# A fused retention and feed-forward kernel: v of chunk 0 loaded and cast by GpSimd's queue, q and k by the two hardware queues, and attention products issued batch by batch instead of grouped in pairs by tiling mode

## Chip, cores, metric

One core of one Trainium2 chip. The metric is the device time of the kernel in microseconds; lower is better. The engines are called as in the profile: PE is TensorE, DVE VectorE, ACT ScalarE, POOL GpSimd, SP SyncE, which here only issues DMAs.

## What is computed

```python
# q, k, v: (4, 8, 768, 64) float32; w_in: (512, 2048); w_out: (2048, 512)
gamma = 1.0 - 2.0 ** (-5.0 - np.arange(H))
for t in range(S):
    state = gamma * state + einsum('bhd,bhe->bhde', k[:, :, t], v[:, :, t])
    y[:, :, t] = scale * einsum('bhd,bhde->bhe', q[:, :, t], state)
x = y.transpose(0, 2, 1, 3).reshape(B * S, H * D)      # 3072 tokens x 512
h = x @ w_in
g = 0.5 * h * (1 + tanh(c * (h + 0.044715 * h ** 3)))  # gelu
out = g @ w_out                                        # 3072 x 512 float32
```

## The kernel before

The recurrence over 768 steps is cut into 6 chunks (index c) of 128 steps, for 4 batches (b). The 8 heads stand as 4 pairs (NHP = 4) of 64 + 64 columns. For a chunk and a batch the work is:

- Load: q, k, v come as 128 x 8 x 64 float32, 256 KB each, in rows of 256 B (load1, L76). prep1 (L135) makes float16 of them: q and k by a product with a decay column, v by a cast.
- T: mm_T (L178) transposes q and k of the 4 pairs by 8 plain 128x128 products into one PSUM bank, and ev_T (L187) copies it to SBUF.
- A: mm_A (L192) makes k q^T per head: 8 products with 64 rows of contraction each, "64*128" in the profile, the two heads of a pair on the two halves of the array's rows, into two banks. ev_A (L206) multiplies both by a decay mask on DVE.
- Y: the carry products (mm_yc, L213) multiply q by the state, 4 plain products; the inner products (mm_yi, L228) multiply A by v, 8 products of 64 columns each, "128*64", the two heads on the two halves of the array's columns, into the same bank. ev_Y (L241) copies it to xT, the transposed input of the feed-forward part.
- S: mm_s (L246), 4 plain products k^T v, and ev_S (L259), which adds the decayed state; decay (L275) is a product on POOL.

The feed-forward part of a chunk takes all 512 tokens. moe1 (L361) makes one block of 128 hidden units with 4 products over the contraction, then a gelu on ACT; moe1_two (L366) puts two blocks of at most 256 tokens into one bank and gives both to one gelu. In chunks 0 and 1, where the tokens of only some batches are there yet, moe1_two is used on 128 or 256 tokens at a time. moe2 (L385) accumulates 16 products per batch into one bank; ev_O (L390) copies it out and stores it, for the last batch by DVE and SP, for the others by ACT.

The order is written out by hand, and each engine runs its instructions in that order. PSUM's 8 banks are shared by tags: "h" 2, "o" 2, "att" 4 (L173). A tile is given a bank of its tag that is free in program order.

- Chunk 0 is written line by line (L427 to L493), with spin (L109), products on zeros, between the pieces. The loads of its 12 tiles are spread over SP and ACT (L90 to L100, L427, L428, L435). w_in is loaded by POOL's queue, which casts it to float16, right behind the k product of batch 2 (L452); hold (L86) keeps the loads of chunk 1 back until a block of w_in is there.
- Chunk 1's attention stands among the feed-forward units of chunks 0 and 1 (L533 to L568).
- From chunk 2 on, run (L417) calls the units of a stage and, after given units, the pieces of attention listed for them. att_AY (L294) groups two batches: carry products of both, A of the next two batches, inner products of both. The S products come later, by att_S.

```python
for b in bs:   mm_yc(c, b, tag)
for b in abs_: mm_A(ca, b)
for b in bs:   mm_yi(c, b)
```

Of the kernel before, what the change touches and what calls it, by code (L numbers as in the profile page):

```python
# [16 lines left out]
def kernel(  # L17
# [37 lines left out]
    att = ctx.enter_context(tc.tile_pool(name="att", bufs=4))  # L55
# [34 lines left out]
    nc.sync.dma_start(out=cst[:, :OT + 128], in_=cst_h.ap())  # L90
    load1(nc.scalar, "q", 0, 0)
    load1(nc.sync, "k", 0, 0)
    load1(nc.scalar, "v", 0, 0)
# [3 lines left out]
    load1(nc.sync, "v", 0, 1)  # L97
    load1(nc.sync, "k", 0, 2)
    load1(nc.sync, "q", 0, 3)
    load1(nc.sync, "v", 0, 3)  # L100
# [8 lines left out]
    def spin(n):  # L109
        ps = bank("o", shape=(128, 512), name="spin_ps")  # L110
        for _ in range(n):
            nc.tensor.matmul(  # L112
                out=ps, lhsT=zero[:, 0:128], rhs=zero, start=True, stop=True
            )
# [3 lines left out]
    nc.gpsimd.memset(st, 0.0)  # L118
# [13 lines left out]

    h16 = {}
# [37 lines left out]


    BANKS = {"h": 2, "o": 2, "att": 4}  # L173

    def bank(tag, dt=F32, shape=(128, NHP, 128), name="ps"):
        return psum.tile(list(shape), dt, tag=tag, bufs=BANKS[tag], name=name)

    def mm_T(c, b):  # L178
        ps = bank("att", F16, (128, 2, NHP, 128), "qkT_ps")
        for i, nm in ((0, "q"), (1, "k")):  # L180
            for hp in range(NHP):
                nc.tensor.transpose(  # L182
                    out=ps[:, i, hp], in_=pair(h16[nm, c, b], hp), identity=iden
                )
        pss["T", c, b] = ps
# [6 lines left out]
    def mm_A(c, b):  # L192
        t = qkT[c, b]
        ps = [bank("att", name=f"a_ps{j}") for j in range(2)]
# [18 lines left out]
    def mm_yc(c, b, tag):  # L213
        y_ps = pss["Y", c, b] = bank(tag, name="y_ps")
        if c == 0:
            return

        for hp in range(NHP):
            nc.tensor.matmul(  # L219
                out=y_ps[:, hp],  # L220
                lhsT=st[:, hp, b],
                rhs=qkT[c, b][:, 0, hp],
                start=(hp == 0),
                stop=False,
                skip_group_check=True,
            )

    def mm_yi(c, b):  # L228
        y_ps = pss["Y", c, b]
        for hp in range(NHP):  # L230
            for j in range(2):
                nc.tensor.matmul(  # L232
                    out=y_ps[j * 64:(j + 1) * 64, hp],
                    lhsT=h16["v", c, b][:, 2 * hp + j],
                    rhs=a_sb[c, b, j][:, hp],
                    start=(c == 0),
                    stop=True,
                    skip_group_check=True,
                )

# [5 lines left out]
    def mm_s(c, b, tag="att"):  # L246
        if c + 1 >= NCk:
            return
        s_ps = pss["S", c, b] = bank(tag, name="s_ps")
        for hp in range(NHP):  # L250
            nc.tensor.matmul(  # L251
                out=s_ps[:, hp],
                lhsT=pair(h16["k", c, b], hp),
                rhs=pair(h16["v", c, b], hp),
                start=True,
                stop=True,
            )

    def ev_S(c, b, eng=nc.vector):  # L259
# [3 lines left out]
        for j in range(2):  # L263
            sl = slice(j * 64, (j + 1) * 64)
            if c == 0:
                copy_on(eng, st[sl, :, b, sl], s_ps[sl, :, sl])
            else:
                eng.tensor_tensor(  # L268
# [15 lines left out]
    def att_T(c, *bs):  # L284
        for b in bs:
            mm_T(c, b)
            ev_T(c, b)

    def att_S(c, b, tag="att"):
        mm_s(c, b, tag)  # L290
        ev_S(c, b)
        decay(c, b)

    def att_AY(c, bs, tag, ca, abs_, eng):  # L294


        for b in bs:
            mm_yc(c, b, tag)
        for b in abs_:
            mm_A(ca, b)  # L300
        for b in bs:
            mm_yi(c, b)
        if tag == "o":
            for b in abs_:
                ev_A(ca, b)
        for b in bs:
            ev_Y(c, b, eng)
        if tag != "o":
            for b in abs_:
                ev_A(ca, b)  # L310
# [30 lines left out]
    def moe1_mm(c, fc, out, t0, t1):  # L341
        wi, wr = w_in_of[fc]
        for kc in range(NHP):
            nc.tensor.matmul(  # L344
                out=out,
# [4 lines left out]
                skip_group_check=True,  # L350
            )

    def g_tile(c, fc):
        if (c, fc // 2) not in g_sb:
            g_sb[c, fc // 2] = gp.tile([128, 2, B * C], F16, tag=f"g{fc // 2}", name="g")
        return g_sb[c, fc // 2]

    def gelu(out, in_):
        nc.scalar.activation(out=out, in_=in_, func=AF.Gelu_apprx_tanh, scale=1.0)  # L359

    def moe1(c, fc):  # L361
        h_ps = bank("h", shape=(128, B * C), name="h_ps")
        moe1_mm(c, fc, h_ps, 0, B * C)
        gelu(g_tile(c, fc)[:, fc % 2], h_ps)

    def moe1_two(c, fp, t0, t1):  # L366

        h_ps = bank("h", shape=(128, 2, B * C // 2), name="h_ps")
        for r in range(2):
            moe1_mm(c, 2 * fp + r, h_ps[:, r, 0:t1 - t0], t0, t1)  # L370
        gelu(g_tile(c, 2 * fp)[:, :, t0:t1], h_ps[:, :, 0:t1 - t0])
# [3 lines left out]
    def moe2_mm(ps, c, b, fcs, n0, n1):  # L375
        for fc in fcs:
            nc.tensor.matmul(  # L377
                out=ps[:, n0:n1],
                lhsT=g_sb[c, fc // 2][:, fc % 2, b * C:(b + 1) * C],
# [5 lines left out]
    def moe2(c, b, fcs):  # L385
        if fcs[0] == 0:
            o_ps[c, b] = bank("o", shape=(128, d_model), name="o_ps")
# [13 lines left out]
    def moe2_last(c, b):  # L401
# [4 lines left out]
        for i in range(2):  # L406
            ps = bank("h", shape=(128, d_model), name="o_ps")
# [9 lines left out]
    def run(units, after):  # L417
        for i, u in enumerate(units):
            u()
            for f, *args in after.get(i, ()):  # L420
                f(*args)
# [5 lines left out]
    load1(AC, "q", 0, 2)  # L427
    load1(AC, "v", 0, 2)  # L428
# [3 lines left out]
    prep1(AC, "v", 0, 0)  # L432
# [10 lines left out]
    prep1(AC, "v", 0, 1)  # L443
    spin(2)
    mm_yc(0, 0, "o")
    mm_yi(0, 0)
    mm_s(0, 0, "h")
# [13 lines left out]
    ev_T(0, 2, AC)  # L461
    prep1(VE, "q", 0, 3)
    mm_yc(0, 1, "o")
    mm_yi(0, 1)
    mm_s(0, 1, "h")
    ev_Y(0, 1, AC)
    prep1(AC, "v", 0, 2)
    prep1(AC, "v", 0, 3)
    ev_S(0, 0, AC)
# [5 lines left out]
    mm_yc(0, 2, "o")  # L475
    mm_yi(0, 2)
    mm_s(0, 2)
    ev_Y(0, 2, AC)
    ev_S(0, 1, AC)
    mm_A(0, 3)  # L480
    ev_A(0, 3)
    moe1_two(0, 0, 0, half)
    mm_yc(0, 3, "o")
    mm_yi(0, 3)
    mm_s(0, 3)
# [3 lines left out]
    moe1_two(0, 1, 0, half)  # L489
    for fp in range(2):  # L490
        moe1_two(0, fp, half, 2 * half)
# [8 lines left out]
    for b in range(B):  # L500
        load1(SY, "q", 1, b)
        load1(SY, "k", 1, b)

# [13 lines left out]


    def att_A(c, b):
        mm_A(c, b)  # L520
        ev_A(c, b)

    def att_Y(c, b):
        mm_yc(c, b, "o")
        mm_yi(c, b)
        mm_s(c, b, "o")
        ev_Y(c, b, AC)

    def end_S(c, b):
        ev_S(c, b)  # L530
        decay(c, b)

    att_T(1, 0)  # L533
    moe1(0, NF - 1)
    prep1(AC, "v", 1, 0)
    att_A(1, 0)
    spin(3)
    att_Y(1, 0)
    att_T(1, 1)
    end_S(1, 0)  # L540
    moe1_two(1, 0, 0, C)
    prep1(AC, "v", 1, 1)
    att_A(1, 1)
    for fp in range(1, 4):
        moe1_two(1, fp, 0, C)
    att_Y(1, 1)
    moe1_two(1, 4, 0, C)
    prep1(AC, "v", 1, 2)
    moe1_two(1, 0, C, half)
    att_T(1, 2)  # L550
    end_S(1, 1)
    moe1_two(1, 1, C, half)
    att_A(1, 2)
    moe1_two(1, 2, C, half)
    moe1_two(1, 3, C, half)
    prep1(AC, "v", 1, 3)
    att_Y(1, 2)
    moe1_two(1, 4, C, half)
    att_T(1, 3)
    end_S(1, 2)  # L560
    moe1_two(1, 5, 0, half)
    att_A(1, 3)
    moe1_two(1, 6, 0, half)
    moe1_two(1, 7, 0, half)
    att_Y(1, 3)
    end_S(1, 3)
    for fp in range(NF // 2):
        moe1_two(1, fp, half, 2 * half)  # L568


    def units2(c, b, n=4):
        u = [(lambda i=i: moe2(c, b, range(i, i + n))) for i in range(0, NF, n)]
        last = u[-1]
        u[-1] = lambda: (last(), ev_O(c, b))
        return u

    for b in range(B):
        prep(2, b)
    u = [units2(0, b, NF // 2) for b in range(B)]
    run(  # L580
        [u[0][0], u[1][0], u[0][1], u[1][1], u[2][0], u[3][0], u[2][1], u[3][1]],
        {
            1: [(att_T, 2, 0), (load, 3, 0)],
            2: [(att_T, 2, 1), (load, 3, 1)],
            4: [(att_AY, 0, (), "o", 2, (0, 1), None), (load, 3, 2)],
            5: [(att_T, 2, 2), (load, 3, 3)],
            6: [(att_T, 2, 3)],
        },
    )
    for b in range(B):  # L590
        prep(3, b)
    run(
        [x for b in range(B) for x in units2(1, b)],
        {
            1: [(att_AY, 2, (0, 1), "h", 2, (2, 3), AC)],
            4: [(att_S, 2, 0), (load, 4, 0)],
            5: [(att_S, 2, 1), (load, 4, 1)],
            7: [(att_T, 3, 0)],
            8: [(att_T, 3, 1), (load, 4, 2)],
            10: [(att_AY, 2, (2, 3), "h", 3, (0, 1), AC), (load, 4, 3)],  # L600
            12: [(att_S, 2, 2)],
            13: [(att_S, 2, 3)],
        },
    )

    for c in range(2, NCk - 1):
        n = c + 1
        more = n + 1 < NCk
        after = {
            1: [(att_T, n, 2)],  # L610
            3: [(att_T, n, 3)],
            8: [(att_AY, n, (0, 1), "o", n, (2, 3), VE)],
            11: [(att_S, n, 0)],
# [55 lines left out]
```

## Time and profile before

| | us |
|---|---|
| median of 3 runs | 223.31 (223.24, 223.31, 224.55) |
| the profiled execution | 224.55 |
| its span in the profile | 222.8 |
| PE busy | 212.7 (95%) |
| ACT busy | 87.9 (39%) |
| POOL busy | 78.9 (35%) |
| DVE busy | 71.9 (32%) |
| first feed-forward product starts | 18.20 |
| first product with w_out starts | 57.23 |

The span is cut into stages by what PE does: attention of chunk 0 to 18.2 us; the first product (w_in) of chunk 0 to 34.3; the attention and first product of chunk 1 to 57.2; the second product (w_out) of chunk 0 to about 75; that of chunk 1, in which most of chunk 2's attention stands, to 92.8; then one stage per chunk of some 33.7 us, 31.4 where no attention follows. In the profile, a line of the timeline is a run of equal instructions: start, time from the first start to the last end, engine, source line, operands, number. Ends of matmuls are modelled, so work is read from start to start.

### The profile page before, as it was taken

To read this page: it belongs to the slowest core of one execution; us is meant where nothing else is said; L and a number is where in the kernel's file an instruction comes from. 1 tells how busy PE (TensorE), PEld (TensorE's weight loads), DVE (VectorE), ACT (ScalarE), POOL (GpSimd) and SP (SyncE) were. 2 spreads that over 40 slices of the span, in tenths; PEclk is the share of its full clock that TensorE was granted. 3 is DMA by queue.
4 is the path that set the end of the run, shared out by engine and by line. 5 is a ranking of instruction groups with operands and counts; after the bars stand their busy time and mean duration, and the time that the engine had idled before them with its cause. 6 is when DMAs were issued, how large, how long until landed. Compare 5 with 4: busy or idle time off the path is not lost.

```text
span 222.8 us, 4048 instructions
## 1 busy us (share of the span) xinstructions
PE 212.7 (95%) x1667; PEld 118.8 (53%) x1667; DVE 71.9 (32%) x132; ACT 87.9 (39%) x154; POOL 78.9 (35%) x91
## 2 busy tenths in 40 slices
PE   7697998899999999999999999999999999999993
PEld 3356446778645556555455555455455445444452
DVE  3466016551025445526324425323425100100001
ACT  2384665655312122254512255512154513367120
POOL 3493365709876770660750794000000000000000
PEclk9999999999999999999999999999999999999999
DMA  7999999999999999999811110011110011200112
GB/s 168 288 190 207 207 264 207 143 190 226 240 240 283 237 297 244 270 258 225 181 50 47 47 47 3 0 50 47 47 49 3 0 47 50 96 0 0 47 50 94
DMA packets 83011, 29.74 MB, mean 133 GB/s; under 512 B 75568, under 2 KB 80048, under 8 KB 82992
## 3 DMA queue, kind: packets, MB, share of 16 engines
q1 hardware_dynamic: 65776, 17.94, 34.4%
q0 software_dynamic: 4224, 4.19, 11.8%
q10 hardware_dynamic: 12992, 7.34, 10.8%
q8 instruction: 13, 0.21, 0.4%
q14 instruction: 6, 0.05, 0.1%
HBM read 27.37 MB, written 6.29 MB: 151 GB/s over the span
## 4 chain that ended last, share of the span: by engine, by line
PE 81%; DMA 8%; SPq 4%; DVE 2%; ACT 1%; issue 1%; POOL 0%; ACTq 0%; DVEq 0%
PE h_ps L344 36%; PE o_ps L377 33%; PE qkT_ps L182 4%; SPq L77 4%; DMA k<-in_k_dram 3%; PE y_ps L232 3%; DMA w_in<-in_moe_w_in_dram 3%; PE a_ps L197 2%; DMA q<-in_q_dram 2%; PE s_ps L251 2%; PE y_ps L219 2%; DVE a_sb L210 1%; DMA out_dram<-o_sb 1%; ACT g L359 1%; POOL k L145 0%
## 5 line engine op out<-in xcount | busy, mean ns | idle before, releaser
L344 PE MATMUL h_ps<-xT,w_in 128*128 128x512 f16 (+2 forms) x504 | 88.2, 329 | 1.6 <-DMA w_in<-in_moe_w_in_dram 1.2
L377 PE MATMUL o_ps<-w_out,g 128*128 128x512 f16 (+1 forms) x400 | 87.7, 371 | 0.3 <-ACT o_sb L398 0.3
L359 ACT ACTIVATE g<-h_ps 128x512 f16<-128x512 f32 (+1 forms) x101 | 58.1, 576 | 55.7 <-PE h_ps L344 55.6
L344 PEld LDWEIGHTS <-w_in 128*128 128x128 f16 x504 | 45.2, 98 | 36.3 <-DMA w_in<-in_moe_w_in_dram 1.4
L377 PEld LDWEIGHTS <-g 128*128 128x128 f16 x400 | 37.9, 98 | 39.0 <-issue 0.3
L210 DVE TENSOR_TENSOR a_sb<-a_ps,mask 128x512 f16<-128x512 f32 x48 | 30.2, 684 | 31.4 <-PE a_ps L197 31.3
L169 DVE COPY qkT<-qkT_ps 128x1024 f16<-128x1024 f16 x21 | 14.5, 691 | 51.1 <-PE qkT_ps L182 51.1
L145 POOL TENSOR_TENSOR k<-k,cst 128x512 f16<-128x512 f32 x24 | 25.3, 1056 | 11.8 <-DMA k<-in_k_dram 11.8
L398 ACT COPY o_sb<-o_ps 128x512 f32<-128x512 f32 x18 | 10.5, 585 | 47.6 <-PE o_ps L377 44.0
L277 POOL TENSOR_TENSOR stg<-st,cst 128x512 f32<-128x512 f16 x16 | 16.4, 1037 | 26.0 <-DVE st L268 25.9
L145 POOL TENSOR_TENSOR q<-q,cst 128x512 f16<-128x512 f32 x20 | 20.9, 1044 | 6.0 <-DMA q<-in_q_dram 4.5
L167 ACT CAST xT<-y_ps 128x512 f16<-128x512 f32 x17 | 9.5, 588 | 17.4 <-PE y_ps L232 13.0
L268 DVE TENSOR_TENSOR st<-s_ps,stg 64x256 f16<-64x256 f32 x32 | 13.5, 421 | 7.5 <-PE s_ps L251 6.9
L395 DVE COPY o_sb<-o_ps 128x512 f32<-128x512 f32 x5 | 3.5, 691 | 23.3 <-PE o_ps L377 23.3
L182 PEld LDWEIGHTS <-q 128*128 128x128 f16 x96 | 7.2, 98 | 6.0 <-issue 0.9
L182 PE MATMUL qkT_ps<-iden,q 128*128 128x128 f16 x96 | 9.3, 219 | 0.9 <-DMA iden<-rr_ident 0.6
L142 POOL CAST v<-v 128x512 f16<-128x512 f32 x16 | 9.8, 609 | 0.9 <-DMA v<-in_v_dram 0.8
L182 PE MATMUL qkT_ps<-iden,k 128*128 128x128 f16 x96 | 9.3, 220 | 0.7 <-POOL k L145 0.7
L232 PE MATMUL y_ps<-a_sb,v 128*64 128x128 f16 x192 | 9.3, 223 | 0.7 <-DVE a_sb L210 0.5
L112 PE MATMUL spin_ps<-zero 128*128 128x512 f16 x27 | 8.3, 445 | 1.2 <-DVE zero L104 1.2
L197 PE MATMUL a_ps<-qkT 64*128 64x128 f16 x192 | 8.2, 218 | 1.2 <-DVE qkT L169 0.7
L411 DVE COPY o_sb<-o_ps 128x256 f32<-128x256 f32 x1 | 0.4, 424 | 25.2 <-PE o_ps L377 25.2
(29 smaller groups left out, 76.0 us busy)
## 6 DMA issues: line engine op xcount, KB each, us to landing
k<-in_k_dram SPq DMA_DIRECT2D x22, 256.0 KB, 4.6
q<-in_q_dram SPq DMA_DIRECT2D x22, 256.0 KB, 4.5
v<-in_v_dram SPq DMA_DIRECT2D x18, 256.0 KB, 4.7
out_dram<-o_sb ACTq DMA_DIRECT2D x18, 256.0 KB, 2.0
w_in<-in_moe_w_in_dram POOLq DMA_DIRECT2D x4, 512.0 KB, 8.6
w_out<-in_moe_w_out_dram POOLq DMA_DIRECT2D x4, 512.0 KB, 9.3
v<-in_v_dram ACTq DMA_DIRECT2D x6, 256.0 KB, 5.5
out_dram<-o_sb SPq DMA_DIRECT2D x5, 256.0 KB, 2.0
```

The costliest lines, as they stand in the source:

```text
L145: eng.tensor_tensor(out=t, in0=src, in1=cst[:, col:col + H].unsqueeze(2).broadcast_to([128, H, Dh]), op=ALU.mult,)
L169: eng.tensor_copy(out=out, in_=in_)
L182: nc.tensor.transpose(out=ps[:, i, hp], in_=pair(h16[nm, c, b], hp), identity=iden)
L197: nc.tensor.matmul(out=ps[j][:, hp], lhsT=t[j * 64:(j + 1) * 64, 1, hp], rhs=t[j * 64:(j + 1) * 64, 0, hp], start=True, stop=True,)
L210: nc.vector.tensor_tensor(out=s, in0=ps[j], in1=mask[:, j], op=ALU.mult)
L232: nc.tensor.matmul(out=y_ps[j * 64:(j + 1) * 64, hp], lhsT=h16["v", c, b][:, 2 * hp + j], rhs=a_sb[c, b, j][:, hp], start=(c == 0), stop=True,
L268: eng.tensor_tensor(out=st[sl, :, b, sl], in0=s_ps[sl, :, sl], in1=stg[sl, :, b, sl], op=ALU.add,)
L277: nc.gpsimd.tensor_tensor(out=stg[:, :, b], in0=st[:, :, b], in1=cst[:, OG:OG + NHP].unsqueeze(2).broadcast_to([128, NHP, 128]), op=ALU.mult,)
L344: nc.tensor.matmul(out=out, lhsT=w_in_sb[wi][:, kc, wr * 128:(wr + 1) * 128], rhs=xT[c][:, kc, t0:t1], start=(kc == 0), stop=(kc == NHP - ...
L359: nc.scalar.activation(out=out, in_=in_, func=AF.Gelu_apprx_tanh, scale=1.0)
L377: nc.tensor.matmul(out=ps[:, n0:n1], lhsT=g_sb[c, fc // 2][:, fc % 2, b * C:(b + 1) * C], rhs=w_out_sb[fc // (NF // NO)][:, fc % (NF // NO ...
L398: nc.scalar.copy(out=o_sb, in_=ps)
```

## The change

- Chunk 0's v is loaded by POOL's queue straight into float16 tiles (load_v16), four issues on POOL; the four loads of v on SP and ACT and the four casts on ACT go. The loads of q and k of chunk 0 are dealt anew over SP and ACT, and the memset of st moves from POOL to DVE.
- Attention is issued batch by batch: mm_Y holds carry, inner and S products of one batch; A is a piece of its own. From chunk 2 on, std lists twelve pieces per chunk, and zip_units spreads them evenly over the units.
- moe1_two goes: each block of 128 hidden units has its own bank and gelu, in chunks 0 and 1 on 128 or 256 tokens.
- Banks: "h" 3, "o" 2, "att" 3. In chunk 0, the S products of batches 0 to 2 take "h" banks and are copied by DVE; from chunk 2 on y and S take "att" banks and ev_Y runs on DVE. The pool of transposed q and k has 3 buffers instead of 4.
- Chunk 2's attention no longer stands in chunk 0's second product, only in chunk 1's. The loads of chunks 3 and later are issued at other places.

```diff
-    att = ctx.enter_context(tc.tile_pool(name="att", bufs=4))
+    att = ctx.enter_context(tc.tile_pool(name="att", bufs=3))
...
+    def load_v16(c, b):
+        t = h16["v", c, b] = pre.tile([128, H, Dh], F16, tag="v16", name="v16")
+        nc.gpsimd.dma_start(
+            out=t, in_=srcs["v"][b, :, c * C:(c + 1) * C, :].rearrange("h p d -> p h d")
+        )
     load1(nc.scalar, "q", 0, 0)
     load1(nc.sync, "k", 0, 0)
-    load1(nc.scalar, "v", 0, 0)
+    load_v16(0, 0)
     nc.sync.dma_start(out=iden, in_=iden_h.ap())
     load1(nc.sync, "q", 0, 1)
     load1(nc.scalar, "k", 0, 1)
-    load1(nc.sync, "v", 0, 1)
+    load_v16(0, 1)
+    load1(nc.scalar, "q", 0, 2)
     load1(nc.sync, "k", 0, 2)
+    load_v16(0, 2)
     load1(nc.sync, "q", 0, 3)
-    load1(nc.sync, "v", 0, 3)
...
-    nc.gpsimd.memset(st, 0.0)
+    nc.vector.memset(st, 0.0)
...
+    def mm_Y(c, b):
...
+        att_b, o_b, h_b = ("att", 3), ("o", 2), ("h", 3)
+        tag, bufs = o_b if c < 2 else att_b
+        y_ps = psum.tile([128, NHP, 128], F32, tag=tag, bufs=bufs, name="y_ps")
...
+        if c + 1 < NCk:
+            tag, bufs = (h_b if b < 3 else att_b) if c == 0 else (o_b if c == 1 else att_b)
+            s_ps = psum.tile([128, NHP, 128], F32, tag=tag, bufs=bufs, name="s_ps")
...
+    def att_Y(c, b):
+        mm_Y(c, b)
+        ev_Y(c, b)
         ev_S(c, b)
         decay(c, b)
...
+    def moe1(c, fc, t0=0, t1=B * C):
+        h_ps = psum.tile([128, B * C], F32, tag="h", bufs=3, name="h_ps")
...
-    def moe1_two(c, fp, t0, t1):
...
+        todo = pieces(c, "T0 T1 A0 T2 A1 Y0 T3 A2 Y1 A3 Y2 Y3")
+        if c + 1 < NCk:
+            for at, b in ((8, 0), (10, 1), (12, 2), (14, 3)):
+                todo.insert(at, ("P", c + 1, b))
...
+    def zip_units(units, todo, over=None):
+        over = len(units) if over is None else over
+        done = 0
+        for i, u in enumerate(units):
+            u()
+            want = min(len(todo), ((i + 1) * len(todo) + over - 1) // over)
+            while done < want:
+                nm, c, b = todo[done]
+                fn[nm](c, b)
+                done += 1
...
     spin(14)
     prep1(VE, "q", 0, 0)
     prep1(PO, "k", 0, 0)
-    prep1(AC, "v", 0, 0)
+    load_v16(0, 3)
...
+    ev_S(0, 0)
     prep1(VE, "q", 0, 3)
-    mm_yc(0, 1, "o")
-    mm_yi(0, 1)
-    mm_s(0, 1, "h")
+    mm_Y(0, 1)
     ev_Y(0, 1, AC)
-    prep1(AC, "v", 0, 2)
-    prep1(AC, "v", 0, 3)
-    ev_S(0, 0, AC)
     mm_A(0, 2)
     ev_A(0, 2)
...
     mm_A(0, 3)
     ev_A(0, 3)
-    moe1_two(0, 0, 0, half)
+    ev_S(0, 1)
+    moe1(0, 0, 0, half)
+    moe1(0, 1, 0, half)
+    mm_Y(0, 3)
     ev_Y(0, 3)
     ev_S(0, 2)
     ev_S(0, 3)
-    moe1_two(0, 1, 0, half)
-    for fp in range(2):
-        moe1_two(0, fp, half, 2 * half)
+    for fc in range(2, 4):
+        moe1(0, fc, 0, half)
+    for fc in range(4):
+        moe1(0, fc, half, 2 * half)
...
+    units = [(lambda fc=fc: moe1(1, fc, C, half)) for fc in range(10)]
+    units += [(lambda fc=fc: moe1(1, fc, 0, half)) for fc in range(10, NF)]
+    units.insert(8, lambda: prep1(AC, "v", 1, 3))
+    zip_units(units, pieces(1, "T2 s1 A2 y2 T3 s2 A3 y3 s3"))
+    for fc in range(NF):
+        moe1(1, fc, half, 2 * half)
...
+    zip_units([u for b in range(B) for u in units2(1, b)], std(2), 15)
+    for c in range(2, NCk):
+        if c + 2 < NCk:
+            for b in range(B):
+                load(c + 2, b)
+        units = [(lambda fc=fc: moe1(c, fc)) for fc in range(NF)]
+        if c + 1 < NCk:
+            units += [u for b in range(B) for u in units2(c, b)]
+            zip_units(units, std(c + 1), len(units) - 2)
```

In std and zip_units, T, A and Y stand for the pieces of a batch and P for its prep; the lower-case y and s of chunk 1 are Y with its copy on ACT, and S's eviction with the decay.

## The prediction

> **What bounds the kernel now.** I read the engine totals and the 40 slices of the page first, then the waits, then TensorE's timeline. All times are of the profiled execution.
>
> ```profile
> PE 212.7 (95%) x1667; PEld 118.8 (53%) x1667; DVE 71.9 (32%) x132; ACT 87.9 (39%) x154; POOL 78.9 (35%) x91
> PE   7697998899999999999999999999999999999993
> ...
> PEclk9999999999999999999999999999999999999999
> DMA  7999999999999999999811110011110011200112
> ...
> PE 81%; DMA 8%; SPq 4%; DVE 2%; ACT 1%; issue 1%; POOL 0%; ACTq 0%; DVEq 0%
> ```
>
> TensorE is busy in all but about 10 us, at full clock, and the chain that ended last is TensorE for 81%. The gaps lie early. These lines of TensorE's timeline give the start and duration of each piece, and the idle time before it in brackets:
>
> ```profile
> 18.20 1.05 PE L344 MATMUL h_ps<-xT,w_in 128*128 128x256 f16 x8 [1.20 <-DMA w_in<-in_moe_w_in_dram]
> ...
> 44.34 0.38 PE L232 MATMUL y_ps<-a_sb,v 128*64 128x128 f16 x7 [0.30 <-DVE a_sb L210]
> ...
> 46.76 0.40 PE L197 MATMUL a_ps<-qkT 64*128 64x128 f16 x8
> 47.09 1.92 PE L344 MATMUL h_ps<-xT,w_in 128*128 128x256 f16 x16
> ...
> 49.16 0.41 PE L232 MATMUL y_ps<-a_sb,v 128*64 128x128 f16 x8
> 49.51 0.40 PE L251 MATMUL s_ps<-v,k 128*128 128x128 f16 x4
> 50.25 7.15 PE L344 MATMUL h_ps<-xT,w_in 128*128 128x256 f16 x64 [0.35 <-ACT xT L167]
> ...
> 67.77 1.89 PE L377 MATMUL o_ps<-w_out,g 128*128 128x512 f16 x8 [0.29 <-ACT o_sb L398]
> ```
>
> So the first product of the feed-forward part waits for w_in until 18.20; from there TensorE idles for about 2.5 us in all, the last time 0.29 us at 67.77. After that only TensorE's own work counts, and in it the order of the attention products:
>
> ```profile
> 101.45 0.61 PE L219 MATMUL y_ps<-qkT,st 128*128 128x128 f16 x8
> 101.99 0.62 PE L197 MATMUL a_ps<-qkT 64*128 64x128 f16 x16
> 102.54 0.64 PE L232 MATMUL y_ps<-a_sb,v 128*64 128x128 f16 x16
> 103.11 2.76 PE L344 MATMUL h_ps<-xT,w_in 128*128 128x512 f16 x12
> 105.71 0.39 PE L251 MATMUL s_ps<-v,k 128*128 128x128 f16 x4
> 105.94 1.89 PE L344 MATMUL h_ps<-xT,w_in 128*128 128x512 f16 x8
> ```
>
> Read the starts. A plain 128-column product takes 0.22/4 = 0.056 us (s_ps: 105.71 to 105.94), a 512-column one 0.216. The 16 row-tiled A products run two at a time, so 8 x 0.056 = 0.445 us are their work, and they take 0.55; the 16 column-tiled Y products take 0.57 for the same 0.445; and the way into A costs 0.54 - 0.445. So each change of the tiling costs about 0.11 us. The single pieces of chunk 1 say the same: A from 46.76 to 47.09 is 0.33 for 0.22 of work, Y from 49.16 to 49.51 is 0.35 for 0.22.
>
> **What the Trainium skill says.** "TensorEngine Tiling (Array Packing)", section Key Properties: changing the tiling mode, not just the tile, drains the array. The trace agrees, with 0.11 us each. "DMA: Bandwidth & Descriptors", section Issuing engines are not separate DMA queues: all issuers share the same 16 engines; the trace shows these engines full (9) from 5.6 us on. The same page, section Specifications: below 512 B a transfer is under line rate, with read-modify-write; no run here shows a casting load of 256 B rows into 128 B rows. "SBUF — State Buffer", section SBUF: two separate sides: descriptors that GpSimd writes can starve while VectorE holds their shared port; the trace has no such case that I can separate.
>
> **The change, part by part.**
>
> *Attention products by batch (chunks 2 to 5).* The matmuls stay the same in number and shape; only their order changes. Before, two batches stand together: carry products (plain), A of the next pair (rows), inner products (columns), then plain again: 3 changes. There are seven such groups, one with A alone (2) and a last one without A (2): 25 changes. After, each of the 16 batches has A by itself (2 changes) and Y by itself (carry plain, inner by columns, S plain: 2), so 64. 39 more x 0.11 = 4.4 us (0.09 to 0.125 each gives 3.5 to 4.9). All of it is on TensorE, and nothing hides it.
>
> *Do the evictions keep up with 3 att banks instead of 4?* In chunks 3 to 5 one piece comes about every two units of 0.86 us; a piece asks VectorE for 0.69 (T), 1.29 (A, the pair) or 0.69 + 0.86 = 1.55 us (Y and S), all under 1.73. The densest stage is chunk 2, whose 12 pieces all stand in the 16 units of chunk 1's second product, one per unit. I followed it by these durations: T0 and T1 at 0.9 and 1.3 us of the stage, their copies done at 2.1 and 2.8; A0 starts at 2.6 with both banks free, its evictions end at 4.4; A1 at 5.2 needs that bank: free; Y0 at 6.6 has its S bank at 6.4; A2 at 9.6 has its banks at 7.9 and 8.7. No wait. Sum of VectorE there: 15 us of 21. Cost 0.
>
> *Chunk 0: one hidden block at a time.* The h banks go from 2 to 3, but s_ps of batches 0, 1 and 2 now sit in all three, and only batch 0's is evicted when the first product asks (ev_S(0, 1) comes after ev_A(0, 3) on VectorE). So moe1(0, 0) and moe1(0, 1) share one bank, and so does moe1(0, 2); all of TensorE's queue stands behind that wait. With 0.43 us for a 256-column unit and 0.384 us for its gelu (row 128x256), from the first product: unit 0 ends at 0.55, its gelu at 1.03, unit 1 at 1.51, Y(0, 3) at 2.1, then six units, the third and fourth of them again one gelu behind: 4.8 us. Before the same work ends at 4.16 (1.57 + 6 x 0.432). +0.65.
>
> *Chunk 1: single units of 128 columns.* Their gelu is estimated at 0.28 us (0.384 minus half of 0.597 - 0.384) against 0.22 us of TensorE. Scalar's work in the stage grows from 14.0 to 17.6 us, TensorE has some 20. The waits for a_sb keep their times (Y(1, 2) at 44.3, A(1, 3) at 46.8, Y(1, 3) at 48.9), but fewer units fit in front: 16 instead of 18 by 44.9. At the end of S(1, 3), 49.5, three units of 0.43 are left; they cover the 0.35 us that TensorE waits for xT before. The last 16 units start at 50.8 and not 50.25: +0.5 (0.3 to 1.2).
>
> *Chunk 0's loads.* v's four casts (0.62 us each) leave Scalar and its loads leave SP and ACT; GpSimd issues them. A w_in issue takes 0.81 us for some 530 packets; 1,040 packets bound it at 0.8 to 1.6 us. Three issues, to 5.5 us at most, lie ahead of k(0, 0), which lands at 5.93 anyway; the 1.8 us memset of st goes to VectorE, idle until 2.62. The fourth fits between the k products of batches 0 and 1 (6.97 to 8.74). k(0, 2), whose landing at 11.59 sets the issue of w_in at 12.57, has one load fewer ahead of it on SP; that gains at most some 1 us at the 288 GB/s of this slice. Against this, k(0, 0) shares with three queues and may be 0.7 us later, and VectorE gets ev_S(0, 0), 0.84 us, before q(0, 3). The engines were full, and the same rows are read, so w_in lands about as early: 17.3 to 18.3, I take 17.8 (-0.4). If a casting packet costs twice the 18.6 ns of an SP packet (34.4% of 16 x 222.8 us over 65,776), 64 packets per engine and load add 1.2 us per load: up to +4.8.
>
> *Chunk 0's second product.* Attention of chunk 2 no longer stands in it, and the issue of the first store waits for a load of chunk 2 instead of chunk 3: the 0.29 us at 67.77 goes. Its 64 products cover the loads of chunk 2. Loads (3, 2) and (3, 3) now stand behind a store on SP, until about 73 us, but are first needed some 20 us later: 0.
>
> Sum: 4.4 + 0.65 + 0.5 - 0.4 - 0.3 = 4.85. The profiled execution took 224.55 (span 222.8 and 1.75 around it) and would take 229.4. It was the slowest of three; on the median, 223.31, this gives 228.2.
>
> **Rivals.**
> 1. *Slow start* (0.12): the casting loads cost double at the engines, or their issue takes over 2 us and holds the k products on GpSimd. +2.4 to +4.8 more: 230.6 to 233. For: 128 B rows. Against: engines move rows of 256 B at 288 GB/s already.
> 2. *Evictions become the bound* (0.08): in chunk 2 or chunk 1 each piece finds its bank 0.2 us late, 12 times: 230.6. For: one bank less, 3.6 us more on Scalar in chunk 1. Against: the ledger above has 0.2 us or more to spare at nearly each piece.
> 3. *Not slower* (0.08): the start is limited by hardware issue (SP needs 1.4 to 2.4 us for its fifth to eighth issue) and not by the engines. A third issuer then lets k(0, 2) land earlier, and w_in with it. It decides if k(0, 2) lands by 6.8 us instead of 11.59: then 4.8 us come back, 223.4. Against: 4.2 MB must be read before w_in's first block is in, and 13 us would need more than the 297 GB/s of the fastest slice.
>
> The main case has 0.72 and 226.3 to 229.8 by itself (changes 3.5 to 4.9, start -1.2 to +1, chunks 0.7 to 2). The range adds the slow start's and the evictions' lower half: 225.9 to 231.0. About 1% (2.2 us) is what a measurement here can tell from no change. Slower by over 1%: 0.92; within: 0.05; faster: 0.03.
>
> **What would show it.** A profile of the changed kernel should have a_ps and y_ps in eights with 0.33 and 0.35 us from start to start; two stages of chunks 3 and 4 at 34.8 us instead of 33.7; the first h_ps near 17.8; three pauses of 0.3 to 0.5 us for gelu right behind it; no wait for att banks after 76 us. I am wrong if the stages of chunks 3 and 4 keep 33.7 us, if the first h_ps is before 15 or after 20 us, or if TensorE waits on VectorE in chunk 2.

## The result, and the profile after

| | before | after |
|---|---|---|
| median, us | 223.55 (223.24 to 224.55, 4 runs) | 230.25 (229.87 to 230.84, 4 runs) |
| profiled execution, us | 224.55 | 230.33 |
| its span | 222.8 | 228.6 |

The ratio is 1.0294, 95% interval 1.0254 to 1.0335: slower by 6.7 us on the medians, where the forecast was 228.2 (225.9 to 231.0). Executions with a granted clock of 0.99 instead of 1.00 occur with several of the kernels below and take some 1.6 us longer (225.23 against 223.67 in the mean of 51 runs of the kernel before), so medians at full clock are given too where the number of such executions matters. First the page of the changed kernel: its engine totals, TensorE's row of the 40 slices, and the shares of the chain that ended last.

```profile
PE 218.5 (96%) x1667; PEld 118.3 (52%) x1667; DVE 82.3 (36%) x147; ACT 82.9 (36%) x161; POOL 80.4 (35%) x94
...
PE   7688998989999999999999999999999999999994
...
PE 89%; DMA 5%; DVE 3%; issue 1%; POOL 0%; ACT 0%; DVEq 0%
```

The number of products is the same (1667), and TensorE is busy for 5.8 us more, 1.0 of it in the products on zeros of the start (8.3 us before, 9.3 after). So most of the time is not in waits that the profile marks; it is in the time that TensorE's own work takes. Cutting both profiles at the same places of TensorE's timeline, start to start, says where:

| stage | before | after | difference | forecast |
|---|---|---|---|---|
| to the first h_ps | 18.20 | 19.15 | +0.95 | -0.4 |
| from there to T(1, 0) | 13.68 | 14.50 | +0.82 | +0.65 |
| from there to the first o_ps | 25.35 | 25.68 | +0.33 | +0.5 |
| from there to the last chunk's first o_ps | 147.99 | 151.90 | +3.91 | +4.1 |
| from there to the end | 17.58 | 17.37 | -0.21 | 0 |

The cuts that are not shown elsewhere, before and then after, T(1, 0) and the last chunk's first o_ps:

```profile
31.88 0.39 PE L182 MATMUL qkT_ps<-iden,q 128*128 128x128 f16 x4
...
205.22 14.02 PE L377 MATMUL o_ps<-w_out,g 128*128 128x512 f16 x80
```

```profile
33.65 0.39 PE L183 MATMUL qkT_ps<-iden,q 128*128 128x128 f16 x4
...
211.23 14.02 PE L352 MATMUL o_ps<-w_out,g 128*128 128x512 f16 x80
```

TensorE's timeline of the changed kernel (start, duration, idle time before in brackets):

```profile
19.15 0.61 PE L332 MATMUL h_ps<-xT,w_in 128*128 128x256 f16 x4
20.23 0.60 PE L332 MATMUL h_ps<-xT,w_in 128*128 128x256 f16 x4 [0.47 <-ACT g L341]
...
104.92 0.39 PE L227 MATMUL y_ps<-qkT,st 128*128 128x128 f16 x4
105.24 0.41 PE L237 MATMUL y_ps<-a_sb,v 128*64 128x128 f16 x8
105.58 0.40 PE L250 MATMUL s_ps<-v,k 128*128 128x128 f16 x4
...
109.81 0.40 PE L201 MATMUL a_ps<-qkT 64*128 64x128 f16 x8
110.14 1.90 PE L332 MATMUL h_ps<-xT,w_in 128*128 128x512 f16 x8
```

A alone takes 110.14 - 109.81 = 0.33 us and Y's column part 0.34, against 0.33 and 0.35 in the forecast; no line after 51 us has an idle time in brackets. The two lines at 19.15 and 20.23 are the pause for a gelu.

The first row of the table went the wrong way. The chain of the changed kernel tells how its start is bound (start, duration, what):

```profile
7.41 8.92 DMA k<-in_k_dram
...
16.41 1.05 POOL k L153
...
17.50 0.41 PE qkT_ps L183 x4
...
18.01 0.70 DVE qkT L177
...
18.75 0.40 PE a_ps L201 x8
19.15 0.62 PE h_ps L332 x4
```

Before, the chain ran through w_in. Now it runs through k of batch 3: its load took 8.9 us and landed at 16.34, and its product (on GpSimd), transpose, copy and A stand in a row up to the first h_ps.

### The profile page after: what moved, and what is told of

Same layout as the page of the kernel before. It is cut to its first block, busy times and chain, and to the rows that moved or that the text cites. A ratio compares the mean times of both kernels' runs of the same rounds, so it can differ in the third digit from the quotient of the medians.

```text
span 228.6 us, 4059 instructions
## 1 busy us (share of the span) xinstructions
PE 218.5 (96%) x1667; PEld 118.3 (52%) x1667; DVE 82.3 (36%) x147; ACT 82.9 (36%) x161; POOL 80.4 (35%) x94
## 3 DMA queue, kind: packets, MB, share of 16 engines
q0 software_dynamic: 8384, 4.72, 15.0%
## 4 chain that ended last, share of the span: by engine, by line
PE 89%; DMA 5%; DVE 3%; issue 1%; POOL 0%; ACT 0%; DVEq 0%
PE o_ps L352 36%; PE h_ps L332 36%; PE qkT_ps L183 4%; DMA k<-in_k_dram 4%; PE y_ps L237 3%; PE a_ps L201 3%; PE spin_ps L122 2%; PE s_ps L250 2%; PE y_ps L227 2%; DVE a_sb L214 1%; DVE qkT L177 1%; DMA out_dram<-o_sb 1%; POOL k L153 0%; DVE st L269 0%; DVE o_sb L386 0%
## 5 line engine op out<-in xcount | busy, mean ns | idle before, releaser
L332 PE MATMUL h_ps<-xT,w_in 128*128 128x512 f16 (+2 forms) x504 | 90.0, 328 | 0.5 <-ACT g L341 0.5
L341 ACT ACTIVATE g<-h_ps 128x512 f16<-128x512 f32 (+2 forms) x126 | 61.9, 496 | 55.9 <-PE h_ps L332 54.6
L332 PEld LDWEIGHTS <-w_in 128*128 128x128 f16 x504 | 44.6, 98 | 33.8 <-issue 0.9
L214 DVE TENSOR_TENSOR a_sb<-a_ps,mask 128x512 f16<-128x512 f32 x48 | 30.9, 686 | 24.6 <-PE a_ps L201 24.5
L177 DVE CAST xT<-y_ps 128x512 f16<-128x512 f32 x17 | 11.8, 692 | 28.3 <-PE y_ps L237 27.1
L237 PE MATMUL y_ps<-a_sb,v 128*64 128x128 f16 x192 | 11.2, 225 | 1.2 <-DVE a_sb L214 1.2
L201 PE MATMUL a_ps<-qkT 64*128 64x128 f16 x192 | 9.5, 219 | 1.3 <-ACT qkT L175 0.7
L201 PEld LDWEIGHTS <-qkT 64*128 64x128 f16 x192 | 5.4, 94 | 10.1 <-issue 6.8
L122 PE MATMUL spin_ps<-zero 128*128 128x512 f16 x27 | 9.3, 489 | 1.2 <-DVE zero L114 1.2
```

The lines of the kernel that those rows point to most:

```text
L122: nc.tensor.matmul(out=ps, lhsT=zero[:, 0:128], rhs=zero, start=True, stop=True)
L177: eng.tensor_copy(out=out, in_=in_)
L201: nc.tensor.matmul(out=ps[j][:, hp], lhsT=t[j * 64:(j + 1) * 64, 1, hp], rhs=t[j * 64:(j + 1) * 64, 0, hp], start=True, stop=True,)
L214: nc.vector.tensor_tensor(out=s, in0=ps[j], in1=mask[:, j], op=ALU.mult)
L237: nc.tensor.matmul(out=y_ps[j * 64:(j + 1) * 64, hp], lhsT=vv[:, 2 * hp + j], rhs=a_sb[c, b, j][:, hp], start=(c == 0), stop=True, skip_gr ...
L332: nc.tensor.matmul(out=h_ps[:, t0:t1], lhsT=w_in_sb[wi][:, kc, wr * 128:(wr + 1) * 128], rhs=xT[c][:, kc, t0:t1], start=(kc == 0), stop=(k ...
```

## The experiments

Theory A: the bulk is changes of tiling on TensorE. Its rival is the new placement with one att bank less. Theory B: the start is lost in chunk 0's loads. Its rival is the new order of evictions in chunk 0.

**1. Tiling changes alone.** In att_AY of the kernel before, for groups with two batches on both sides:

```diff
-        for b in bs: mm_yc(c, b, tag)
-        for b in abs_: mm_A(ca, b)
-        for b in bs: mm_yi(c, b)
+        for b, ab in zip(bs, abs_):
+            mm_yc(c, b, tag)
+            mm_A(ca, ab)
+            mm_yi(c, b)
```

> The kernel before, with the seven full groups of chunks 2 to 5 issued as carry, A, inner for one batch and then carry, A, inner for the other: 6 changes of tiling per group instead of 3, so 46 instead of 25, with the same products, banks and copies in the same places. Theory (each change costs TensorE about 0.108 us): 21 x 0.108 = 2.3 us more, about 225.8 us, and a group goes from 1.66 to 1.98 us. Rival (the time after was lost because pieces stand apart and wait for banks and copies, not by the changes themselves): within 0.4 us of the kernel before.

Measured: 226.14 against 223.54, ratio 1.0106 (1.0078 to 1.0135). The second kernel keeps the carry products together and alternates half batches:

```diff
+        for b, ab in zip(bs, abs_):
+            for hps in (range(2), range(2, 4)):
+                mm_A(ca, ab, hps)
+                mm_yi(c, b, hps)
```

> The kernel before, with A and inner products of each full group interleaved by half batches (four A products, four inner products, and so on): 9 changes of tiling per group instead of 3, so 67 instead of 25, close to the 64 of the changed kernel. Theory: 42 x 0.108 = 4.5 us more, about 228.0 us, twice the step of the kernel with 46 changes; a group goes from 1.66 to 2.31 us. If a change straight from rows to columns is cheaper than one by way of plain products, it stays below 4 us. Rival (placement and banks): within 0.4 us of the kernel before.

Measured: 228.08 against 223.54, ratio 1.0196 (1.0167 to 1.0225). The first group of each in TensorE's timeline, in the kernel before, then with 46 changes and with 67:

```profile
75.57 0.61 PE L219 MATMUL y_ps<-qkT,st 128*128 128x128 f16 x8
...
77.23 2.76 PE L377 MATMUL o_ps<-w_out,g 128*128 128x512 f16 x12
```

```profile
74.62 0.39 PE L219 MATMUL y_ps<-qkT,st 128*128 128x128 f16 x4
74.94 0.40 PE L197 MATMUL a_ps<-qkT 64*128 64x128 f16 x8
75.27 0.41 PE L232 MATMUL y_ps<-a_sb,v 128*64 128x128 f16 x8
75.61 0.40 PE L219 MATMUL y_ps<-qkT,st 128*128 128x128 f16 x4
...
76.61 2.76 PE L383 MATMUL o_ps<-w_out,g 128*128 128x512 f16 x12
```

```profile
74.24 0.61 PE L220 MATMUL y_ps<-qkT,st 128*128 128x128 f16 x8
74.78 0.29 PE L199 MATMUL a_ps<-qkT 64*128 64x128 f16 x4
75.00 0.30 PE L233 MATMUL y_ps<-a_sb,v 128*64 128x128 f16 x4
75.23 0.28 PE L199 MATMUL a_ps<-qkT 64*128 64x128 f16 x4
...
76.58 2.76 PE L384 MATMUL o_ps<-w_out,g 128*128 128x512 f16 x12
```

The same products take 1.66 us before (75.57 to 77.23), 1.99 with three changes more, 2.34 with six more: 0.11 us for each, also for a change straight from rows to columns. The stage with the feed-forward part of chunk 2, in which such a group stands twice, goes from 33.65 to 34.33 and 35.01 us: 6 x 0.113 and 12 x 0.113. The changed kernel has 16 changes there instead of 6, and its stage is 34.75: 10 x 0.110. Banks, copies and places were those of before, so the rival of theory A, which allowed 0.4 us, is out, and the time follows the number of changes.

**2. The loads alone, and without them.** The kernel before with the loads of chunk 0, their casts and the memset of st as changed:

```diff
-    load1(nc.scalar, "v", 0, 0)
+    load_v16(0, 0)
...
+    load1(nc.scalar, "q", 0, 2)
...
-    prep1(AC, "v", 0, 0)
+    load_v16(0, 3)
```

> The kernel before with the change of chunk 0's loads alone: v through GpSimd's queue with the cast, no casts of v on Scalar, q and k dealt as in the changed kernel, the memset of st on VectorE. Theory (k of batches 2 and 3 land later because the engines take longer for the same rows): the first h_ps starts at 18.9 to 19.3 instead of 18.20, and the whole takes 0.6 to 1.1 us more, about 224.4. Rival (the start was lost to the new order of evictions in chunk 0, ev_S of batch 0 on VectorE ahead of q of batch 3, not to the loads): the first h_ps at 17.9 to 18.3, 223.2 to 223.7.

Measured: 225.40 against 223.52, ratio 1.0069 (1.0043 to 1.0095), first h_ps at 19.29. The changed kernel with the old loads is the other side:

> The changed kernel with the loads and v casts of chunk 0 as before (and the memset of st on GpSimd), everything else as changed. Theory (loads are worth 0.9 us of the difference, the changes of tiling 4.2, chunks 0 and 1 about 1.2): the first h_ps at 18.0 to 18.4 us, the whole 0.7 to 1.1 us less than the changed kernel, about 229.3. Rival (the new order of evictions): no more than 0.3 us less, 230.0.

Measured: 228.93 against 223.52, ratio 1.0229 (1.0196 to 1.0262), first h_ps at 16.99. From the changed kernel's 1.0294 that is 0.0065 x 223.5 = 1.5 us. So the loads cost 1.5 to 1.9 us, about twice the 0.9 expected, and theory B's rival is out.

Why more than the 0.95 us of the table? The first h_ps of four profiles whose code is equal up to there (before, the two kernels of experiment 1 and b_one_block below) starts at 18.20, 17.44, 17.06 and 17.64. The profile of before, on which the forecast stood, had the latest start of them, and was the slowest of its runs. (The four were not all taken on the same chip; 17.06 and 17.44 were.)

**3. The cast, or the place in the queues?** With v as float32 through the same queue at the same places, and the casts on Scalar as before:

```diff
     def load_v16(c, b):
-        t = h16["v", c, b] = pre.tile([128, H, Dh], F16, tag="v16", name="v16")
-        nc.gpsimd.dma_start(out=t, in_=srcs["v"][...])
+        load1(nc.gpsimd, "v", c, b)
```

> As the kernel before with the changed loads, but v goes through GpSimd's queue as float32, and Scalar casts it as before. If the cast in the transfer is what costs (a packet of GpSimd's casting queue takes 30 ns by the profile's queue table, one of the hardware queues 18 ns): the start comes back to about 18.2 us and the whole to 223.3 to 223.8. If the third queue or the new deal of q and k over the two hardware queues is what delays k of batches 2 and 3: it stays at 18.9 to 19.3 us, about 224.4.

Measured: 224.15 against 223.52, ratio 1.0027 (1.0008 to 1.0045), first h_ps at 17.81. Most of the loss is gone. The ratio leaves 0.6 us, the medians at full clock (223.91 against 223.47) 0.4. The DMA queues in the first 12 us (packets, MB, share of 16 engines): before, then with the casting loads, then with the uncast ones. q0 is GpSimd's queue, the others the two hardware queues.

```profile
q1 hardware_dynamic: 5425, 1.40, 51.6%
q10 hardware_dynamic: 5478, 1.38, 50.9%
```

```profile
q0 software_dynamic: 2857, 0.36, 46.2%
q1 hardware_dynamic: 3578, 0.94, 46.1%
q10 hardware_dynamic: 3120, 0.79, 31.0%
```

```profile
q1 hardware_dynamic: 4448, 1.16, 43.3%
q10 hardware_dynamic: 3455, 0.87, 32.2%
q0 software_dynamic: 309, 1.02, 23.5%
```

A hardware packet of 256 B takes 51.6% of 16 x 12 us over 5,425, 18.3 ns; a casting packet 46.2% of it over 2,857, 31 ns, and writes 128 B. These are the packets' own times, and they overlap: with the casting loads the three shares add up to 123%. What they take from each other shows in the rate. From 8 to 12 us 4,576 packets were moved before, 14 ns of each engine for one, and 3,501 with the casting loads, 1,678 of them casting; if a hardware packet still took 14 ns, that is an estimated 23 ns for a casting one. In the 12 us the hardware queues moved 2.78 MB before, v's among them, and 1.73 with the casting loads. That leaves open whether it is the engine time as such, or v ahead of q and k. So the next two issue the same loads later:

```diff
-    load_v16(0, 1)
     load1(nc.scalar, "q", 0, 2)
     load1(nc.sync, "k", 0, 2)
-    load_v16(0, 2)
...
     prep1(PO, "k", 0, 0)
-    load_v16(0, 3)
+    load_v16(0, 1)
...
     prep1(PO, "k", 0, 1)
+    load_v16(0, 2)
+    load_v16(0, 3)
```

> The kernel before with the changed loads of chunk 0, casting, but GpSimd issues v of batch 1 only behind its k product of batch 0, and v of batches 2 and 3 behind that of batch 1. If the cost of the changed loads is engine time of the casting packets (31 ns each against 18.3 ns, 4,096 of them, 3.3 us on each of 16 engines), a later issue saves little: about 225 us, first h_ps at 18.7 to 19.3. If it is that v stands ahead of q and k at the engines: about 223.8, first h_ps by 18.0.

Measured: 223.18 against 223.67, ratio 0.9972 (0.9954 to 0.9991), first h_ps at 17.17.

> The same later issue, but v goes through GpSimd's queue as float32 and is cast on Scalar. With the loads uncast and early the time was 0.6 us above the kernel before, with T of batch 1 waiting until 10.73 us for q. If v ahead of q(0, 1) was the reason, this returns to the kernel before or below: 222.9 to 223.5. If the third queue itself costs: 224.1 again.

Measured: 223.47 against 223.67, ratio 0.9976 (0.9953 to 0.9999), first h_ps at 16.55. And the changed kernel with the casting loads in these later places:

> The changed kernel, where GpSimd issues v of batch 1 behind its k product of batch 0, and v of batches 2 and 3 behind that of batch 1; the loads still cast. If v's early place at the engines is what costs the start (the kernel before with the changed loads took 225.4, with the later issue 223.18): about 2 us less than the changed kernel, 228.0 to 228.7, first h_ps at 16.8 to 17.4 instead of 19.15. If the casting packets' engine time costs wherever they stand: 229.5 to 230.3, first h_ps at 18.5 or later.

Measured: 228.54 against 223.61, ratio 1.0230 (1.0210 to 1.0251), first h_ps at 17.37: as little as with the old loads. GpSimd's timeline of the kernel before, of the changed one, then of this one:

```profile
11.59 1.04 POOL L145 TENSOR_TENSOR k<-k,cst 128x512 f16<-128x512 f32 x1 [1.52 <-DMA k<-in_k_dram]
```

```profile
1.25 2.83 POOL L96 DMA_DIRECT2D v<-in_v_dram  x3 [0.81 <-POOLq L581]
...
6.87 0.94 POOL L96 DMA_DIRECT2D v<-in_v_dram  x1
...
12.51 1.04 POOL L153 TENSOR_TENSOR k<-k,cst 128x512 f16<-128x512 f32 x1 [3.63 <-DMA k<-in_k_dram]
13.50 1.56 POOL L312 DMA_DIRECT2D w_in<-in_moe_w_in_dram  x2
16.41 1.04 POOL L153 TENSOR_TENSOR k<-k,cst 128x512 f16<-128x512 f32 x1 [1.36 <-DMA k<-in_k_dram]
```

```profile
1.25 1.08 POOL L96 DMA_DIRECT2D v<-in_v_dram  x1 [0.80 <-POOLq L581]
...
8.28 1.81 POOL L96 DMA_DIRECT2D v<-in_v_dram  x2
10.29 1.04 POOL L151 TENSOR_TENSOR k<-k,cst 128x512 f16<-128x512 f32 x1 [0.20 <-DMA k<-in_k_dram]
11.28 1.56 POOL L310 DMA_DIRECT2D w_in<-in_moe_w_in_dram  x2
13.16 1.04 POOL L151 TENSOR_TENSOR k<-k,cst 128x512 f16<-128x512 f32 x1 [0.32 <-DMA k<-in_k_dram]
```

The same 4,096 casting rows are moved in both. Issued later, they let k of batch 2 in 2.2 us earlier (10.29 for 12.51), w_in's issue with it, and k of batch 3 by 3.2 us. So issuing v early, beside q and k, is the cause, and the cast makes it dearer: 1.9 us early and cast, 0.4 to 0.6 early and uncast, none late, either way. The new deal of q and k over the hardware queues, which all these kernels share, costs nothing, as the late ones show. The Trainium skill, "DMA: Bandwidth & Descriptors", section Queues, rings and completion order, says that each engine goes round the queues that have work, packet by packet; this fits the counts: from 8 to 10 us the three queues of the kernel with the casting loads moved 723 (GpSimd's), 503 and 519 packets, where before the two hardware queues moved 1,110 and 1,173. That turns are what delays q and k is argued from this: the page's packet can hold several descriptors, and no run here watches a single engine.

**4. Chunks 0 and 1.** The S product of batch 2 is moved out of the third h bank of the changed kernel:

```diff
-            tag, bufs = (h_b if b < 3 else att_b) if c == 0 else ...
+            tag, bufs = (h_b if b < 2 else att_b) if c == 0 else ...
```

> The changed kernel, with the S product of batch 2 of chunk 0 put in an att bank instead of the third h bank. Theory (the first hidden blocks share one bank, and the second waits 0.47 us for the first one's gelu): the pause between the first two units goes, the first product of chunk 0 shrinks from 14.5 to about 14.0 us, the whole by 0.3 to 0.6 us, to about 229.8. Rival (the att bank is now late for the products of batch 3 in its place, or the later gelus hold TensorE anyway): no gain, 230.1 to 230.6.

Measured: 230.14 against 223.54, ratio 1.0293 (1.0261 to 1.0324): by its time not to be told from the changed kernel. TensorE's timeline tells more:

```profile
19.09 1.05 PE L332 MATMUL h_ps<-xT,w_in 128*128 128x256 f16 x8
20.07 0.24 PE L237 MATMUL y_ps<-a_sb,v 128*64 128x128 f16 x1
20.53 0.38 PE L237 MATMUL y_ps<-a_sb,v 128*64 128x128 f16 x7 [0.22 <-DVE a_sb L214]
```

The pause of 0.47 us is gone, and a wait of 0.22 us for a_sb, which it had covered, stands right behind. From the first h_ps to the third unit it is 1.99 instead of 2.19 us, and from the first h_ps to T(1, 0) 14.16 instead of 14.50, which is also what a_old_loads and a_cast_late take. The shared bank was real and worth 0.34 us of this stage, but at its line only 0.20 of the 0.47.

Another 0.43 us of the stage's +0.82 have nothing to do with single blocks. Before, TensorE waited 1.20 us for w_in ahead of the first h_ps, and the evictions of A of batch 3 (a_sb) ran under that wait (17.04 to 18.33 us on VectorE). In the kernel b_win_early of experiment 5, which has the blocks of before but no wait for w_in, TensorE waits for a_sb behind the first block instead, and the stage takes 14.11 instead of 13.68.

The single blocks by themselves, in the kernel before:

```diff
-        h_ps = bank("h", shape=(128, 2, B * C // 2), name="h_ps")
         for r in range(2):
-            moe1_mm(c, 2 * fp + r, h_ps[:, r, 0:t1 - t0], t0, t1)
-        gelu(g_tile(c, 2 * fp)[:, :, t0:t1], h_ps[:, :, 0:t1 - t0])
+            h_ps = bank("h", shape=(128, B * C), name="h_ps")
+            moe1_mm(c, 2 * fp + r, h_ps[:, t0:t1], t0, t1)
+            gelu(g_tile(c, 2 * fp)[:, r, t0:t1], h_ps[:, t0:t1])
```

> The kernel before, with each hidden block of chunks 0 and 1 in a bank and gelu of its own on the same 128 or 256 tokens, instead of two blocks to a bank; everything else as before. Theory (this part of the change costs TensorE 0.7 to 1.1 us by waits for gelus and inner products in chunks 0 and 1, by the traces of before and after): 0.6 to 1.3 us more, about 224.5. Rival (that loss comes from the third h bank's use by S products, not from single blocks): within 0.3 us of the kernel before.

Measured: 226.31 against 223.67, ratio 1.0097 (1.0062 to 1.0132), more than either theory said. The end of chunk 1's first product in TensorE's timeline, of this kernel and of the changed one:

```profile
51.12 8.52 PE L344 MATMUL h_ps<-xT,w_in 128*128 128x256 f16 x64 [0.35 <-ACT xT L167]
59.47 0.81 PE L377 MATMUL o_ps<-w_out,g 128*128 128x512 f16 x3
```

```profile
51.03 8.46 PE L332 MATMUL h_ps<-xT,w_in 128*128 128x256 f16 x76
59.33 6.85 PE L352 MATMUL o_ps<-w_out,g 128*128 128x512 f16 x31
```

Here 64 products take 8.35 us, 0.130 each; in the changed kernel 76 take 8.30, 0.109 each, and so do the 64 of before (50.25 to 57.23). With two h banks single blocks of 256 columns hold TensorE back by about a fifth; with the changed kernel's three they don't. (The profile marks no wait for a bank in either; the comparison says it.) So this run overstates what single blocks cost in the changed kernel, and the +0.82 and +0.33 of the table stand on the traces alone, where they repeat: a_old_loads and a_cast_late have 14.50 and 25.68 too.

**5. A faster start for the kernel before.**

```diff
     prep1(VE, "q", 0, 2)
-    prep1(PO, "k", 0, 2)
     load_w_in(0)
+    prep1(PO, "k", 0, 2)
     load_w_in(1)
```

> The kernel before, with the first w_in block issued by GpSimd ahead of the k product of chunk 0's batch 2 instead of behind it (about 10.1 us instead of 12.57). Theory (TensorE waits 1.2 us for that block while the DMA engines stand nearly idle from 13.2 to 15 us): the first h_ps starts at 17.0 to 17.4 instead of 18.20, and the whole takes 222.6 to 223.0. Rival (the block takes engine time from k of batches 2 and 3, and attention ends later by as much): 223.3 or more.

Measured: 222.97 against 223.54, ratio 0.9971 (0.9961 to 0.9981); TensorE no longer waits for w_in:

```profile
16.71 1.05 PE L344 MATMUL h_ps<-xT,w_in 128*128 128x256 f16 x8
```

The chain to the first h_ps now comes through k of batch 3, whose load lands at 14.03 us, and the attention behind it. Joined with the late, uncast v:

> The kernel before with v uncast through GpSimd's queue, issued late, and the first w_in block ahead of the k product of batch 2. Uncast, v went as 256 packets of 4 KB instead of 4,096 of 256 B, in 2.8 instead of 4.7 us of each engine, so w_in and k(0, 3) should land earlier than in the kernel with the early block alone (222.97): first h_ps at 15.8 to 16.6, the whole 222.0 to 222.7. Rival (attention of chunk 0 is a chain of its own by then): 16.7 again and no gain over 222.97.

Measured: 223.54 against 223.67, ratio 0.9992 (0.9958 to 1.0027), first h_ps at 17.32 with 0.30 us of waiting for w_in again. The runs scatter from 222.86 to 226.24; the median at full clock is 223.15 against 223.62, so the gain of the early block may be there, but none beyond it. w_in's first issue stands at 10.12 us there, behind three v loads of its own queue, and at 9.04 in the kernel with the early block alone; that this is why was not tried. The version with the early w_in block alone beats both kernels, by 0.3% and 3.2%; the late casting loads alone (0.9972) are as good.

## Why the prediction was right or wrong

The direction was right, and 230.25 lies within the range of 225.9 to 231.0, but above the 226.3 to 229.8 of the forecast's main case: it is inside only because the range took in the lower half of the rivals. The terms one by one:

- *Tiling changes, +4.4 us.* Right in mechanism and size. 39 changes at the 0.11 of experiment 1 are 4.3 us. From the first o_ps to that of the last chunk the changed kernel takes 3.91 us more than the profile of before; without what that profile had extra there (0.35, see the 0.29 us wait below), 4.26, or 0.109 per change. The feed-forward stages of chunks 2 and 3 (the forecast named them by the attention of chunks 3 and 4 in them) take 34.75, forecast 34.8.
- *Evictions keep up with three att banks, 0.* Right: TensorE has no wait after 51 us, in chunk 2's dense stage neither.
- *Chunk 0, one block at a time, +0.65.* The shared bank was where it was said to be, and the stage grew by 0.82. Of the three pauses only the first shows as one (0.47). Experiment 4 puts the bank itself at 0.34 us, since a_sb was next in line, and 0.43 on the wait for a_sb that the wait for w_in had covered in the profile of before. The forecast counted the waits of one resource without asking what stood behind each. That its 0.65 and 0.5 for chunks 0 and 1 add up to the measured 1.15 is luck.
- *Chunk 1, single units, +0.5.* Measured 0.33. With two h banks, in b_one_block, this stage takes 27.57 us instead of 25.35; the forecast did not see that the third bank saves this.
- *Chunk 0's loads, -0.4.* Wrong, and the one step of the wrong sign. It read: "The engines were full, and the same rows are read, so w_in lands about as early". Full engines were the reason why the deal matters. v is needed last of the three, and three of its loads were put on a third queue from 1.25 us on, beside the q and k that the chain needs first. k(0, 2) had "one load fewer ahead of it on SP" and its product still started 0.9 us later than in the profile of before (12.51 for 11.59), 1.6 to 2.2 us later than in the other three with the same start (10.88, 10.54 and 10.33), since what was ahead of it at the engines was not what was ahead of it on SP. The cast made a packet's time 31 ns, 1.7 times a hardware one (1.6 by the rates) and not twice, and was no cost where it stood late. The forecast's 18.6 ns was such a packet time too; at the 288 GB/s of the trace a row takes an engine 14 ns. On the medians this step is +1.5 to +1.9, so it was mis-sized by some 2 us, close to the lower end of the rival called slow start, whose mechanism, engine time or issue time of the casts, is only part of it: the same casts issued late cost nothing.
- *The 0.29 us wait, -0.3.* It is gone, but it was no fixed cost of before. The stage it lies in takes 35.56 us in the profile of before (57.23 to 92.79) and 35.21 in the four profiles of b_loads, b_cast_late, b_win_early and b_one_block, which have the same code there (58.66 to 93.87 in the first). One execution's wait was counted as the kernel's.
- *From profile to median.* The forecast took 1.2 us off for the profile of before being its slowest run, and did not ask in which stage. It was mostly the start, the stage in which the changed loads then lost; so the table shows +0.95 for what costs 1.5 to 1.9.

Together: 4.3 for changes, 1.5 for the loads as taken out of the changed kernel, 1.15 for chunks 0 and 1, gives 6.95, of 6.7 measured. The 0.2 less at the end goes with the loads (17.3 to 17.4 us in every profile in which GpSimd loads v of chunk 0, 17.5 to 17.6 in the others; why is not shown). The forecast's 4.85 was short of this by 2.1: 1.9 for the loads and 0.3 for the wait, less 0.1 for the changes.

## What to carry to other kernels

Where TensorE is the bound, count the changes of tiling mode in its order and price them from the trace; keeping two batches' row and column products together is worth about 0.11 us per change saved, and nothing else has to move. When a start is bound by transfers, look at which rows the chain needs first and what shares the engines with them, across all queues: a third queue is no free road, and issuing the least urgent load early takes from the urgent ones. The length of a wait in the profile is not what its removal gives at that place (0.20 of 0.47 us here); ask what is late next.

## What the runs showed of the hardware that was not expected

- Uncast float32 rows of 256 B on GpSimd's queue go as 4 KB packets: the whole run has 4,544 packets on that queue instead of the 4,224 of before, 320 more for 1 MB of v; as casting loads v adds 4,160 there (8,384), and the hardware queues lose 4,160 when v leaves them. By the size classes of the profile's page 256 of the 320 are of 2 to 8 KB. The Trainium skill, "DMA: Bandwidth & Descriptors", section SWDGE vs HWDGE vs iDMA, says that a packet is preferably of at most 4,096 B; the uncast rows reach that, and with the cast each packet is one row, 128 B written.
- The packets of that queue take 23.5% of 12 us for 1.02 MB, 2.8 us of each engine, and slices with them reach 408 GB/s; in hardware packets 1.05 MB takes 3.6 us at the 288 GB/s of the kernel before. (The 4.7 us in the expectation of b_v_best are packet times, which overlap.) It gave no time here: issued late, cast and uncast loads do equally well.
- The start of one and the same code varies by over 1 us between executions: the first h_ps at 17.06, 17.44, 17.64 and 18.20 us in four profiles. The stage that begins at 92.79 us before, by contrast, takes 33.65 us in that profile and in those of b_loads, b_cast_late, b_win_early and b_one_block.
